# Chunks 2 and 3 of a gated recurrence take the split form and leave through memory, and three chunks' loads get an earliest time

## The chip, the cores and the metric

The kernel runs on one core of one Trainium2 chip. The metric is device time in microseconds for one execution. The unchanged kernel takes 480.79 us (median of three runs, 479.53 to 482.15). A core has TensorE (PE; its weight loads are shown as PEld), VectorE (DVE), ScalarE (ACT), GpSimd (POOL) and SyncE (SP), whose queue issues every DMA of this kernel. Each engine runs its own instructions in the order in which the program emits them.

## The reference

Two blocks follow each other. The first is a recurrence over 768 tokens for 4 batches x 8 heads, with a 48 x 48 state for each head:

```python
f = 1.0 / (1.0 + np.exp(-f_logit))
for t in range(S):
    state = f[:, :, t, :, None] * state + np.einsum('bhd,bhe->bhde', k[:, :, t], v[:, :, t])
    y[:, :, t] = np.einsum('bhd,bhde->bhe', q[:, :, t], state)
```

Its output, 3072 tokens x 384, is the input x of the second:

```python
a = x @ w1          # 384 x 1024
b = x @ w2
h = a * b @ w3      # 1024 x 1024
return (h @ w_out)  # 1024 x 384
```

q, k, v and f_logit arrive as 32-bit floats; the weights as 64-bit words.

## The kernel before

**Chunks.** The tokens are cut into 24 chunks of 128 (`NU`), six to a batch; four chunks make a block of 512 tokens, the unit of the FFN. For each chunk, `front` loads f, k and q (two DMAs of 96 KB each) and v (192 KB), takes the sigmoid on ScalarE, runs a forward and a backward product scan on VectorE, and scales q and k by them. TensorE then forms key-query products ("pairs"), ScalarE copies them to SBUF, GpSimd masks them (`affine_select`), TensorE multiplies by v and adds what the state gives, and the state is updated on VectorE.

**Two forms.** Below `NPE` (4) a chunk takes the whole form: 128 x 128 pairs, one select, values and state products over all 128 tokens (`first_values`, with the state copied by ScalarE into block-diagonal tiles `sb`), an update (`first_update`), and x^T made on TensorE with a permutation (`moved`, L737) and settled by ScalarE (L742). From `NPE` on a chunk takes the split form. It is cut at token 64: pairs are made within each half, so half as many products and two selects of 64 partitions each; the second half reads the state at token 64 (`mid`, L617 or L619), and the state at the chunk's end needs a second addition (L622) and the gain (L681). In this form the output leaves through memory: two DMAs write `ys` to a scratch tile in DRAM (`written`, L729) and a third gathers x^T from it (`gathered`, L732).

**Visits.** In the split form TensorE does a chunk in one visit, which also holds the pairs and the update of the next chunk. `begin` does those two for the first split chunk.

**Weights.** The 64-bit words of w1 and w2 (12 pieces of 512 KB), w_out (4 of 768 KB) and w3 (8 of 1 MB) are loaded by SP and turned into 32-bit floats: two operations on ScalarE (L1157, L1160), four on VectorE (L1163, L1164, L1168, L1174, the last of which is called the join). w3 and w_out are then folded into one 1024 x 384 matrix on TensorE (L1221), and after differences of these (L1253, L1267) later blocks use a seven-product scheme for halves. `fetch` describes a piece, `weights` all of them.

**The FFN.** Block 0 comes in parts: tokens of chunks 0 and 1 with the first half of w1 and w2, chunks 2 and 3 with the same, all four with the second half. A product takes one of four PSUM banks (pool "f"); ScalarE copies a's (L796) and VectorE multiplies b's by it (L801), which frees the bank.

**The order of the work.** Nothing is emitted directly. Every step is a task of a planner (`Plan`): an engine, an assumed cost, what it depends on, a priority (lower first), slots that it takes and frees. `order` repeatedly picks the task that can start earliest by the planner's own clock, then by priority, and the tasks are emitted in order of those starts. So each engine's order is the planner's; the chip's own times only decide how long it waits at each step. Loads take one of eight "lanes". SP is a queue in that order too: an issue that waits for data, as a gather does for its write, holds all later ones. Before the planner's time 35 (`FULL`), idle stretches of TensorE are filled with dummy products (`idle`, L268). A chunk's due time (`need`) is 0, 1, 2, 3 for the first four, then 60 and 14.5 more for each further one; f, k and q have priorities of due time minus 30, 29.5 and 29.

**The tail.** The last visit has no next chunk and makes one dummy transpose instead (L654).

Of the kernel before, what the change touches and what calls it, by code (L numbers as in the profile page):

```python
# [45 lines left out]
P = 128  # L46
C = 128
# [10 lines left out]
NB = B * S // TB  # L58
NLEAF = 6
NQ = HP * C  # L60
NPE = 4
NRAW = 3
NF = 4
DH = DM // 2
# [3 lines left out]
HIGH = float.fromhex("0x1.dffffep+16")  # L68
W = C // 2
FULL = 35.0  # L70
FLOOR = 2.0**-60
RANGE = 2.0**-40


class Plan:
# [13 lines left out]

        self.pools[name] = [None] * n  # L90

    def add(self, eng, cost, emit, deps=(), prio=0.0, takes=(), frees=(), lag=0.2, slack=0.0):


        t = {
            "eng": eng, "cost": cost, "emit": emit, "deps": [d for d in deps if d is not None], "prio": prio,
            "takes": list(takes), "frees": list(frees), "lag": lag, "slack": slack, "at": None, "end": None, "no": len(self.tasks),
        }
        self.tasks.append(t)
        return t  # L100

    def order(self):
        free, done, left = {}, [], list(self.tasks)
        enders = {}
        for t in self.tasks:
            for f in t["frees"]:
                enders.setdefault(id(f), []).append(t)

        def after(t, ds):

            if any(d["end"] is None for d in ds):
                return None
            return max([0.0] + [d["end"] + (d["lag"] + t["slack"] if d["eng"] != t["eng"] else 0.0) for d in ds])

        def places(t, name):

            ends = [(after(t, enders[id(h)]) if h else 0.0, i) for i, h in enumerate(self.pools[name])]
            return [e for e in ends if e[0] is not None]

        def start(t):  # L120

            waits, at = list(t["deps"]), free.get(t["eng"], 0.0)
            for name in t["takes"]:
                if name in self.pools:
                    ends = places(t, name)
                    if not ends:
                        return None
                    at = max(at, min(ends)[0])
                    continue
                n, taken = self.slots[name]  # L130
                if len(taken) >= n:
                    waits += enders[id(taken[-n])]
            ready = after(t, waits)
            return None if ready is None else max(at, ready)

        while left:
            at, _, _, t = min(
                ((at, t["prio"], t["no"], t) for t in left if (at := start(t)) is not None), key=lambda x: x[:3]
            )
            t["at"], t["end"] = at, at + t["cost"]  # L140
            free[t["eng"]] = t["end"]
            for name in t["takes"]:
                if name in self.pools:
                    t["got"] = min(places(t, name))[1]
                    self.pools[name][t["got"]] = t
                else:
                    self.slots[name][1].append(t)
            left.remove(t)
            done.append(t)
        return sorted(done, key=lambda t: (t["at"], t["no"]))  # L150
# [44 lines left out]
def ranged(ctx, tc, q, k, f_logit, v, w1, w2, w3, w_out, out, ident, w12, wc, left):  # L195
# [128 lines left out]
    def past(u, n, *names):  # L324
        return [tk[u - n][nm] for nm in names if u >= n and nm in tk[u - n]]

    def moves(n, size, rate, emit, deps, prio, late=0.0):


        for j in range(n):  # L330
            i = plan.add("SP", 0.45, (lambda: None) if j else emit, [d] if j else deps, prio - j * 1e-3, takes=["lane"], lag=0.6)
            d = i
            t = plan.add("DMA", size / n / rate, lambda: None, [i], prio - j * 1e-3, lag=1.3 + late, frees=[i])
        return t
# [5 lines left out]
    def front(u):  # L340

        s, t = st[u], tk[u]
        n0 = need(u)

        def load(dst, src):
            def emit():
                if dst is fs[0] and u == 0:

                    nc.sync.dma_start(dst[0:64], src[u].rearrange("two d n -> (two d) n")[0:64])
                    nc.sync.dma_start(dst[rows(1)], src[u, 1])  # L350
                    return
                for par in range(2):
                    nc.sync.dma_start(dst[rows(par)], src[u, par])
            return emit

        fu, qu, ku = (x[u if u < 4 else u % n] for x, n in ((fs, 2), (qs, 3), (ks, 2)))

        def free(n, *names):

            if u < 4:  # L360
                return []
            return asked[8:9] + [tk[u - n if u - n >= 4 else u % n][nm] for nm in names]

        t["lf"] = moves(2, 197, 250, load(fu, f_logit), free(2, "g"), n0 - 30)
        t["lk"] = moves(2, 197, 250, load(ku, k), free(2, "k"), n0 - 29.5)
        t["lq"] = moves(2, 197, 250, load(qu, q), free(3, "q"), n0 - 29)

        def load_v():
            s["v"] = at(12288 + NQ, DM) if u == 3 else loads.tile([P, DM], F32, name="vt")
            loaded(s["v"], u)  # L370

        t["lv"] = moves(
            1, 197, 320, load_v, [] if u == 3 else past(u, 4 if u in (4, 5, 6) else 3, "v", "s"),
            n0 - (28.2, 28.2, 28.2, 29.6, 12)[min(u, NPE)],
        )

        def gates():
            nc.scalar.activation(gate[u % 2][:, 0:NQ], fu, AF.Sigmoid)  # L378

        t["g"] = plan.add("ACT", 0.65, gates, [t["lf"]] + past(u, 2, "r") + past(u, 3, "G"), n0)  # L380
        if u % NCH and "G" in tk[u - 1]:
            tk[u - 1]["G"]["deps"].append(t["g"])

        def forward():
            s["P"] = one.tile([R, NQ], F32, name="fwd")
            nc.vector.tensor_tensor_scan(s["P"], gate[u % 2][:, 0:NQ], floor, 0.0, ALU.mult, ALU.max)  # L386

        t["p"] = plan.add("DVE", 1.25, forward, [t["g"]] + past(u, 1, "q", "i", "l"), n0)

        def last():  # L390
            nc.scalar.copy(lasts[:, u], heads(s["P"])[:, :, C - 1])  # L391

        t["l"] = plan.add("ACT", 0.2, last, [t["p"]], n0)

        def ends():
            nc.vector.reciprocal(heads(back)[:, :, C - 1], heads(s["P"])[:, :, C - 1])

        t["i"] = plan.add("DVE", 0.18, ends, [t["p"]] + past(u, 1, "r"), n0)

        def scale_q():  # L400
            s["Q"] = work3.tile([R, NQ], F32, name="Q")
            nc.vector.tensor_tensor(s["Q"], qu, s["P"], ALU.mult)

        t["q"] = plan.add("DVE", 0.7, scale_q, [t["p"], t["lq"]] + past(u, 3, "v", "a"), n0 + 0.1)

        def backward():
            s["R"] = one.tile([R, NQ], F32, name="bwd")
            nc.vector.tensor_tensor_scan(  # L408
                s["R"][:, ::-1], gate[u % 2][:, NQ:0:-1], back[:, ::-1], 0.0, ALU.mult, ALU.max
            )  # L410

        t["r"] = plan.add("DVE", 1.25, backward, [t["i"]] + past(u, 1, "k"), n0)

        def scale_k():
            s["K"] = work.tile([R, NQ], F32, name="K")
            nc.vector.tensor_tensor(s["K"], ku, s["R"], ALU.mult)

        t["k"] = plan.add("DVE", 0.7, scale_k, [t["r"], t["lk"]] + past(u, 2, "a", "t"), n0)
        if u in (2, 3):
            t["k"]["frees"].append(coming)  # L420
# [207 lines left out]
    def rest(u):  # L628
# [12 lines left out]
            t["s"] = plan.add("PE", 0.6, lambda: first_update(u), [t["e"], t["lv"]] + past(u, 1, "d"), n0 - 997)  # L641
        else:
            middle(u)
            more = u + 1 < NU
            after = tk[u + 1] if more else {}

            def visit():
                s["py"] = ps.tile([P, 2, NQ], F32, name="py")
                values(u, 1)
                if more:  # L650
                    pairs(u + 1)
                else:
                    s["pa"] = ps.tile([P, 2, NQ], F32, name="pa")
                    nc.tensor.transpose(out=s["pa"][:, 0, 0:R], in_=s["K"][:, 0:C], identity=ident[0:R, 0:R])  # L654
                values(u, 0)
                from_state(u)
                if more:
                    update(u + 1)
# [535 lines left out]
    def weights():  # L1194
        due = {(0, 0): 5.0, (1, 0): 8.0, (0, 1): 24.0, (1, 1): 26.0}
        pieces.update({key: [] for key in due})
        for half in range(2):
            for which, w in enumerate((w1, w2)):
                for kc in range(KM):
# [4 lines left out]
                        [(0, KH * P, w12_part(which, kc, c0), due[which, half] + 0.1 * kc, [])],  # L1204
                    )

        done = []
        for i in range(0, KF, 2):
            src = w_out[i * P : (i + 2) * P].rearrange("(kc p) c -> p kc c", p=P)
# [92 lines left out]

    setup()
    for u in range(NU):
        if u <= NPE:
            front(u)
        if u == NPE:
            turning(u)
            begin(u)
        if u >= NPE and u + 1 < NU:  # L1310
            front(u + 1)
            turning(u + 1)
        rest(u)
        if u == NPE - 1:
            weights()
        if u == NU - 1:
            looked = plan.add("DVE", 1.0, judge, [tk[i]["y"] for i in range(NU)], -20)
            sent = moves(1, 0.4, 250, told, [looked], 0, 20.0)
            judged = plan.add("DVE", 0.2, decided, [moves(1, 0.4, 250, heard, [sent], 0, 20.0)], -20)
# [349 lines left out]
```

## Time and profile before

| | |
|---|---|
| time, median of three runs | 480.79 us (479.53 to 482.15) |
| time of the profiled execution | 481.99 us |
| its span, first to last instruction | 480.3 us |
| mean granted TensorE clock | 0.997 |
| busy: PE, PEld | 466.2, 398.5 us |
| busy: DVE, ACT, POOL | 362.7, 141.2, 63.2 us |
| read from and written to HBM | 40.67 and 8.65 MB |
| chain that ended last, by engine | PE 78%, DMA 8%, DVE 7%, POOL 3% |

The profile is one execution. A line of a timeline gives the start and length of a group of like instructions, its engine, the line of the kernel, the tiles written and read, shapes, how often, and in brackets how long the engine had been idle before it and whom it waited for. A product of 32-bit floats appears as two passes on TensorE, so 72 passes are 36 products. TensorE counts as busy while a product is in flight, so a full row is not a TensorE at its peak. For loads, the queue rows give the issue; the landing is told apart from it.

### The profile page before, as it was taken

Reading aid. Unit: us, or ns where it says so; the run is one execution under the profiler, and the core shown is the slowest. Engines: PE = TensorE matmul, PEld = TensorE weight load, DVE = VectorE, ACT = ScalarE, POOL = GpSimd, SP = SyncE. Lnnn points to the kernel's source line nnn. Section 1 sums busy time; section 2 is a strip of 40 time slices with the busy share of each in tenths; the row PEclk is TensorE's granted clock in tenths of the full one; section 3 lists DMA queues with packets and bytes.
Section 4 is the critical chain, followed back from the end, with each engine's and each line's share of the span. In section 5 each row is a group of like instructions: output and inputs, shape, how many; then the busy total and the mean of one; then the engine's idle time right before and its main releaser. Section 6 shows DMA issues by size and latency. Waiting matters only on the chain.

```text
span 480.3 us, 11336 instructions
## 1 busy us (share of the span) xinstructions
PE 466.2 (97%) x4667; PEld 398.5 (83%) x4667; DVE 362.7 (76%) x706; ACT 141.2 (29%) x310; POOL 63.2 (13%) x88
## 2 busy tenths in 40 slices
PE   8799899999999899999999999999999999999995
PEld 6688644656799788899988889988899888889995
DVE  8999699999999889899899467367653667655541
ACT  4787356472313334333432210010100110110000
POOL 9300000013303224212431100000000000000000
PEclk9999999999999999999999999999999999999998
DMA  6899277843516664455631002100101000000011
GB/s 183 261 386 235 61 256 248 286 139 92 138 38 171 190 185 138 125 150 142 168 111 26 18 18 66 50 17 2 57 27 49 1 0 1 0 2 0 34 66 40
DMA packets 36622, 50.14 MB, mean 104 GB/s; under 512 B 4546, under 2 KB 26050, under 8 KB 35538
## 3 DMA queue, kind: packets, MB, share of 16 engines
q1 hardware_dynamic: 36562, 49.33, 34.1%
q8 instruction: 38, 0.62, 0.6%
q14 instruction: 22, 0.18, 0.1%
HBM read 40.67 MB, written 8.65 MB: 103 GB/s over the span
## 4 chain that ended last, share of the span: by engine, by line
PE 78%; DMA 8%; DVE 7%; POOL 3%; issue 2%; ACT 1%; SPq 0%; ACTq 0%; DVEq 0%; POOLq 0%
PE f L759 62%; PE f L1221 7%; PE py L513 2%; DMA vt<-in_v_dram 2%; DMA place<-in_w_dram 2%; PE pa L439 2%; DMA place<-in_w_out_dram 2%; PE f L453 2%; PE py L532 2%; PE pa L546 2%; DMA k<-in_k_dram 2%; DVE place L1168 1%; DVE place L1174 1%; POOL ab L304 1%; DVE ab L801 1%
## 5 line engine op out<-in xcount | busy, mean ns | idle before, releaser
L759 PE MATMUL f<-xt,w 128*128 128x256 f32 (+1 forms) x600 | 161.1, 397 | 3.4 <-ACT ab L796 1.9
L759 PEld LDWEIGHTS f<-xt,w 128*128 128x128 f32 x600 | 112.9, 190 | 29.1 <-issue 10.0
L759 PE MATMUL f<-place 128*128 128x192 f32 (+1 forms) x504 | 112.1, 349 | 0.1
L759 PEld LDWEIGHTS f<-place 128*128 128x128 f32 x504 | 87.7, 190 | 6.2 <-DVE place L1010 0.4
L569 POOL TENSOR_SCALAR_AFFINE_SELECT A<-A 64x512 f32<-64x512 f32 (+1 forms) x44 | 40.9, 929 | 117.3 <-ACT A L563 107.5
L1221 PE MATMUL f<-place 128*128 128x384 f32 x128 | 42.8, 489 | 0.2 <-DVE place L1174 0.2
L862 ACT COPY a<-f 128x256 f32<-128x256 f32 x36 | 13.4, 373 | 93.2 <-PE f L759 78.0
L1221 PEld LDWEIGHTS f<-place 128*128 128x128 f32 x128 | 23.8, 190 | 16.5 <-DVE place L1174 0.8
L759 PE MATMUL f<-xt,place 128*128 128x256 f32 x144 | 37.3, 382 | 0.0
L759 PE MATMUL f<-wc,ab 128*128 128x192 f32 x192 | 35.2, 327 | 0.0
L759 PEld LDWEIGHTS f<-wc,ab 128*128 128x128 f32 x192 | 32.0, 190 | 0.5
L408 DVE TENSOR_TENSOR_SCAN bwd<-gate,back 112x512 f32<-112x512 f32 x24 | 30.0, 1248 | 0.8
L386 DVE TENSOR_TENSOR_SCAN fwd<-gate,floor 112x512 f32<-112x512 f32 x24 | 29.6, 1232 | 1.2 <-ACT gate L378 0.3
L759 PEld LDWEIGHTS f<-xt,place 128*128 128x128 f32 x144 | 26.6, 189 | 3.3
L886 DVE TENSOR_TENSOR place<-f,a 128x256 f32<-128x256 f32 x36 | 15.2, 423 | 18.3 <-PE f L759 18.0
L1157 ACT ACTIVATE place<-place 128x512 f32<-128x512 f32 (+2 forms) x24 | 21.3, 887 | 7.8 <-DVE w L1174 3.8
L672 POOL TENSOR_TENSOR G<-lasts,gate 112x4 f32<-112x4 f32 x20 | 11.6, 580 | 88.1 <-ACT lasts L391 55.2
L1160 ACT ACTIVATE place<-place 128x512 f32<-128x512 uint32 (+2 forms) x24 | 21.1, 886 | 5.7 <-DMA place<-in_w_out_dram 5.7
L708 ACT ACTIVATE ys<-py 112x512 f32<-112x512 f32 x20 | 11.9, 596 | 34.4 <-PE py L532 34.4
L759 PE MATMUL f<-place,w 128*128 128x256 f32 x72 | 21.4, 379 | 0.0
L897 DVE TENSOR_TENSOR ab<-f,place 128x256 f32<-128x256 f32 x36 | 15.2, 423 | 6.2 <-PE f L759 5.3
L995 DVE TENSOR_TENSOR place<-ab 128x512 f32<-128x512 f32 x24 | 16.9, 703 | 3.5 <-PE f L759 3.5
(126 smaller groups left out, 641.1 us busy)
## 6 DMA issues: line engine op xcount, KB each, us to landing
place<-in_w_dram SPq DMA_DIRECT2D x8, 1024.0 KB, 4.9
place<-in_w_dram SPq DMA_DIRECT2D x12, 512.0 KB, 10.4
out_dram<-o SPq DMA_DIRECT2D x24, 192.0 KB, 1.9
q<-in_q_dram SPq DMA_DIRECT2D x46, 96.0 KB, 2.9
vt<-in_v_dram SPq DMA_DIRECT2D x23, 192.0 KB, 3.8
k<-in_k_dram SPq DMA_DIRECT2D x44, 96.0 KB, 2.3
f<-in_f_logit_dram SPq DMA_DIRECT2D x43, 96.0 KB, 2.5
yt<-ys SPq DMA_DIRECT2D x40, 96.0 KB, 2.6
```

The source lines that it names most:

```text
L386: nc.vector.tensor_tensor_scan(s["P"], gate[u % 2][:, 0:NQ], floor, 0.0, ALU.mult, ALU.max)
L408: nc.vector.tensor_tensor_scan(s["R"][:, ::-1], gate[u % 2][:, NQ:0:-1], back[:, ::-1], 0.0, ALU.mult, ALU.max)
L569: nc.gpsimd.affine_select(out=a, in_=a, pattern=pattern, compare_op=ALU.is_ge, fill=0.0, base=0, channel_multiplier=-1,)
L708: nc.scalar.activation(ys, py, AF.Copy, accum_out=ysum[:, u : u + 1])
L759: nc.tensor.matmul(out_, lhsT=lhs[i], rhs=rhs[i], start=start and i == 0, stop=i == len(lhs) - 1, skip_group_check=True,)
L862: nc.scalar.copy(q["a"], q["X"])
L886: nc.vector.tensor_tensor(ups["u3", k], q["Y"], q["a"], ALU.add)
L897: nc.vector.tensor_tensor(m if which else to(tok, half), q[bank_], m, ALU.add)
L995: nc.vector.tensor_tensor(abs_[j], x, y, op)
L1157: nc.scalar.activation(m, hi.bitcast(F32), AF.Abs)
L1160: nc.scalar.activation(lo.bitcast(F32), lo, AF.Copy, bias=2.0, scale=2.0**-51)
L1221: nc.tensor.matmul(w3s["p", jc], lhsT=w3s[jc][:, kc * P : kc * P + P], rhs=wos[:, kc], start=(kc == 0), stop=(kc == KF - 1),)
```

## The change

Chunks 2 and 3 take the split form: `NPE` becomes 2. They don't share visits: a new constant `SOLO` = 4 takes over what used to hang on the first split chunk. From chunk 4 on a visit includes the next chunk's pairs and update, as before; chunks 2, 3 and 4 each have a `begin` of their own, and the visits of 2 and 3 hold only their own values and state products. By the form's definition, x^T of these two goes through memory, and chunks 1 and 2 no longer copy their state into `sb`. The dummy transpose of the last visit goes.

Tasks get an earliest start, `since`. f, k and q of chunks 5, 6 and 7 get their due time minus 22 (`AHEAD`): 52.5, 67 and 81.5 by the planner's clock.

`weights` is cut in two: the part for w1 and w2 is described after chunk 0, the rest (`folding`) after chunk 3. The loads, their priorities and conditions stay.

```diff
-NPE = 4
+NPE = 2
+SOLO = 4
...
+AHEAD = 22.0
...
-            waits, at = list(t["deps"]), free.get(t["eng"], 0.0)
+            waits, at = list(t["deps"]), max(free.get(t["eng"], 0.0), t["since"])
...
-            i = plan.add("SP", 0.45, (lambda: None) if j else emit, [d] if j else deps, prio - j * 1e-3, takes=["lane"], lag=0.6)
+            i = plan.add("SP", 0.45, (lambda: None) if j else emit, [d] if j else deps, prio - j * 1e-3, takes=["lane"], lag=0.6, since=since)
...
-        t["lf"] = moves(2, 197, 250, load(fu, f_logit), free(2, "g"), n0 - 30)
-        t["lk"] = moves(2, 197, 250, load(ku, k), free(2, "k"), n0 - 29.5)
-        t["lq"] = moves(2, 197, 250, load(qu, q), free(3, "q"), n0 - 29)
+        since = n0 - AHEAD if 4 < u < 8 else 0.0
+        t["lf"] = moves(2, 197, 250, load(fu, f_logit), free(2, "g"), n0 - 30, since=since)
+        t["lk"] = moves(2, 197, 250, load(ku, k), free(2, "k"), n0 - 29.5, since=since)
+        t["lq"] = moves(2, 197, 250, load(qu, q), free(3, "q"), n0 - 29, since=since)
...
-            n0 - (28.2, 28.2, 28.2, 29.6, 12)[min(u, NPE)],
+            n0 - (28.2, 28.2, 28.2, 29.6, 12)[min(u, 4)],
...
-            more = u + 1 < NU
+            more = u + 1 < NU and u >= SOLO
...
                 if more:
                     pairs(u + 1)
-                else:
-                    s["pa"] = ps.tile([P, 2, NQ], F32, name="pa")
-                    nc.tensor.transpose(out=s["pa"][:, 0, 0:R], in_=s["K"][:, 0:C], identity=ident[0:R, 0:R])
                 values(u, 0)
...
+    def folding():
         done = []
...
-        if u <= NPE:
+        if u <= SOLO:
             front(u)
-        if u == NPE:
+        if NPE <= u <= SOLO:
             turning(u)
             begin(u)
-        if u >= NPE and u + 1 < NU:
+        if u >= SOLO and u + 1 < NU:
             front(u + 1)
             turning(u + 1)
         rest(u)
-        if u == NPE - 1:
+        if u == 0:
             weights()
+        if u == 3:
+            folding()
```

## The prediction

> **What bounds the kernel now.** I read the page first (shares and slices), then busy time by stretches of ten microseconds, then the timelines of TensorE, ScalarE and VectorE around the stage that the change touches, then the queue of the loads. From the page, busy time, and VectorE's row of the 40 slices (12 us each, in tenths):
>
> ```profile
> PE 466.2 (97%) x4667; PEld 398.5 (83%) x4667; DVE 362.7 (76%) x706; ACT 141.2 (29%) x310; POOL 63.2 (13%) x88
> DVE  8999699999999889899899467367653667655541
> ```
>
> TensorE is never idle for long, and VectorE is full until about 240 us but for one slice (48 to 60 us). The stretches (busy us of 10 on PE, PEld, DVE, ACT, POOL; clock; DMA share; GB/s):
>
> ```profile
> 30.00:40.00 10.00, 10.00 (x81) 9.03 (x76) 9.67 (x20) 9.26 (x19) 0.00 (x0) 1.00 1.01 318
> 40.00:50.00 10.00, 10.00 (x48) 8.81 (x47) 7.08 (x15) 5.31 (x9) 0.00 (x0) 1.00 0.87 206
> 50.00:60.00 10.00, 8.10 (x32) 5.81 (x32) 7.47 (x17) 4.42 (x9) 0.51 (x1) 1.00 0.19 50
> ```
>
> DMA is saturated to 40 us and nearly so to 48. TensorE's timeline: start, length, line, form, and in brackets the idle time before it.
>
> ```profile
> 33.26 1.60 PE L737 MATMUL f<-ys,ab 112*128 112x128 f32 x12
> 34.70 15.71 PE L759 MATMUL f<-xt,w 128*128 128x256 f32 x72
> 52.30 8.02 PE L759 MATMUL f<-xt,w 128*128 128x256 f32 x30 [1.90 <-ACT ab L796]
> ```
>
> From 34.70 the FFN runs without a break but for 1.90 us before 52.30. Two things set this stage, and neither is TensorE's attention work. VectorE joins the words of w1 and w2, and ScalarE, in order, stands behind a late load. From VectorE's timeline and then ScalarE's:
>
> ```profile
> 37.89 0.69 DVE L1174 CUSTOM_DVE_ANT_0 w<-place,w 128x1024 uint16<-128x1024 uint16 x1
> ...
> 52.28 0.42 DVE L801 TENSOR_TENSOR ab<-f,ab 128x256 f32<-128x256 f32 x1 [4.41 <-ACT ab L796]
> ```
>
> ```profile
> 51.12 0.88 ACT L1160 ACTIVATE place<-place 128x768 f32<-128x768 uint32 x1 [4.89 <-DMA place<-in_w_out_dram]
> 51.90 0.35 ACT L796 COPY ab<-f 128x256 f32<-128x256 f32 x1
> ```
>
> The sixth join (w2's last of the first half) ends at 38.58. The 72 passes take 15.71 us, 0.218 each; four w1 products are 24 passes, 5.24 us, so TensorE first needs w2 at 39.94. Part(0,2), 48 passes, ends at 45.17; 24 more fill the four banks by 50.4. Then it stands until ScalarE, held at L1160 for w_out's second piece, frees one. That piece was issued on SP's queue at
>
> ```profile
> 42.03 0.39 SPq L1138 DMA_DIRECT2D place<-in_w_out_dram  x1
> ```
>
> and landed at about 51.1, behind f and k of chunk 5 (issued at 40.11 and 41.02), with q of 5 and 6 (45.21) among its packets.
>
> **What the Trainium skill says.** "TensorE: Matmul & The Clock Gate", The mechanism: products that use different row groups run side by side. The trace agrees: 32 passes of L439 with 48 rows and 64 columns take 0.47 us, 15 ns each, where a pass of L429 (48 rows, 128 columns) takes about 69. "SBUF — State Buffer", Who interferes with whom: a VectorE instruction with two SBUF inputs contends with a GpSimd one that reads SBUF. It agrees: K at 22.20 (L416) took 1.40 us under the select of 21.90 to 23.05, 0.69 elsewhere. "DMA: Bandwidth & Descriptors", Two DMAs through the same engine are not ordered: a DMA that reads what another wrote must wait on the issuing engine for its completion. The waits agree (SP's queue; total, times, longest), and below it are the page's landings of both moves and the landing of the v loads issued between 12.8 and 28.6 us:
>
> ```profile
> SPq L732 <- DMA yt<-ys: 3.7, 4, 1.7
> ```
>
> ```profile
> yt<-ys SPq DMA_DIRECT2D x40, 96.0 KB, 2.6
> xt<-yt SPq DMA_DIRECT2D x20, 192.0 KB, 3.2
> ```
>
> ```profile
> DMA to landing us min/median/max: 9.3/9.6/10.0
> ```
>
> A move through memory costs 2.6 and 3.2 us on a free queue, but in the weight stage each landing takes nearly 10.
>
> **TensorE's work.** Removed for chunk 3, by starts: pairs 24.34 to 25.44 (1.10), values 29.25 to 30.27 (1.02), state 30.27 to 31.23 (0.96), update 32.66 to 33.26 (0.60), x^T 33.26 to 34.70 (1.44): 5.12 us. In its place stand the products of a later visit, whose ends are
>
> ```profile
> 119.43 0.45 PE L513 MATMUL py<-A,vt 64*64 64x64 f32 x16
> ...
> 121.41 0.91 PE L1221 MATMUL f<-place 128*128 128x384 f32 x2
> ```
>
> that is 1.98 us with the pairs and update of the next chunk, the same content as one chunk's own. The transposes stay. Gain 3.14 per chunk, 6.3 us for two, all before 34.70, where TensorE waits for joins anyway. Priced at nothing beyond an earlier start: w1's third join ends at 32.20, so without chunk 3's x^T in front TensorE could begin up to 2.5 us earlier, but then needs w2 at 37.4, before 38.58. At most 1.36 us (39.94 to 38.58) is to be had, if joins don't move.
>
> **VectorE.** They do move. The state of chunk 2 was 0.35 + 0.36 (L687, L688); it becomes 0.35 + 0.36 + 0.35 (L619, L622, L681): +0.35. Of chunk 3, the first two, 0.71, now come before the joins (its old pair ran at 53.22, after the gate of chunk 4). GpSimd's select was one of 1.1 us, and becomes two of 0.66 to 1.4, each a chance to block a two-input operation: 0 to 0.7 more per chunk. The sixth join moves to 39.64 at least and 41.0 at most, against a need of 39.94: -0.3 to +1.1. I take **+0.4**.
>
> **ScalarE** loses 3.2 us before 35: two pairs of L697 (2 x 0.71), two settles (2 x 0.48), two mask copies at 0.58 for 1.01. It runs ahead of VectorE here: nothing. The end-of-kernel transpose of L654 (0.3) goes: within the tail, nothing.
>
> **x^T through memory.** Chunk 3's Q would end near 24.9 (24.2 + 0.7 for chunk 2's state). Then pairs and update 1.1, ScalarE 0.6, selects 1.3 to 2.8, visit 1.1, ys 0.8: 29.8 to 31.3. The write lands 2.6 to 10 us later, the gather 3.2 to 5 after that: x(3) at 35.6 to 46.3. Part(2,4) needs it at 45.17 + 0.4 = 45.6. Cost 0 to 0.7; I take **+0.2**. The cover is part(0,2), 10.4 us of TensorE; without it every microsecond counts whole. Behind the waiting gather on SP stand w1/w2's last pieces, f and k of chunk 4, and w_out: these are late next.
>
> **The loads.** f and k of chunk 5 before w_out's second piece, q of 5 and 6 among it: 8 x 96 KB = 768 KB go out of this stage (f of 6 and 7, at 52.81, go later too). Into it come 4 x 96 + 2 x 192 = 768 KB of yt and xt. At 206 to 318 GB/s either is 2.5 to 3.8 us: a wash in bytes. What is left is when SP issues: a hold at the gathers costs, a lighter queue afterwards gives. I put the landing between 47 and 55, against 51.1. The stall then changes by -1.9 (TensorE is never held) to +4 (each microsecond of lateness is one of TensorE's). I take **-0.9**, since the transfer is issued with nothing of chunk 5 in front. Chunk 5's gate feeds a scan at 93.53 and its f would be on chip before 60: the later loads are priced at nothing, covered by some 30 us; past that cover lateness would stop VectorE.
>
> **After 55.** The products and folds are the same, at TensorE's pace; VectorE, which arrives together with it at fold two (83.69, 0.17 idle), has up to 4.4 us of freed idle time and 1.1 of added work: nothing. The order is planned anew from end to end, so stalls such as 1.37 us at 161.25 may go or new ones come: -1.5 to +1.5, taken at **-0.2**.
>
> Sum: 0.4 + 0.2 - 0.9 - 0.2 = -0.5 us on the profiled execution of 481.99 (span 480.3 and 1.7 around it), which is 1.2 above the median of 480.79. From the median: **480.3 us**.
>
> **Rivals.** A, the forecast: the saved TensorE time lies in front of VectorE's joins and buys nothing, the bytes cancel; 478.4 to 483.2. B, the late piece is the bound and the lighter queue frees it: landing by 49 takes all 1.9, the start up to 1.3 more, and 161.25's stall up to 1.4: 476.2 to 478.4, centre 477.5. For it: 4.41 us of idle VectorE time in the same place; against it: the same bytes come back. C, slower: SP stands at the gathers. With the write issued near 26 and landing near 36, SP holds from about 29; the last w2 piece slips from 29.88 to 36 or 37, w_out's second from 42.03 to about 46, its landing to 55: the stall is 1.9 + 4, time 484.8. It decides from a landing after 53.5 (2.4 us late). For it: the ten-microsecond landings; against it: the held queue drains, so what follows lands faster. D, the later loads are already late in the order and nothing moves there: then B fails, A or C stands; inside their chances.
>
> **Chances.** A 0.40, B 0.26, C 0.34; half a per cent, 2.4 us, is about what this kernel's measurement tells from no change. So faster 0.26, same 0.40, slower 0.34. The range takes in most of B and C and leaves about one in ten out at each end: 476.5 to 486; A alone, 478.4 to 483.2.
>
> **What would show it.** Right: L737 x24 for x48 with four more gathers and eight writes; first FFN product within a microsecond or two of 34.7; VectorE still over 9.5 of 10 to 48 us; ScalarE's wait on w_out between 3 and 7 us. Wrong: an FFN start below 32 (the joins were not the gate), that wait gone (B), or longer, with SP's waits for yt at 10 us in total (C); or a new stall of over 2 us past 55, which I price at nothing.

## The result and the profile after

The changed kernel takes **483.33 us** (median of 11 runs, 481.11 to 485.32), the kernel before 479.59 (11 runs, 478.15 to 482.15). The ratio is 1.0084 with a 95% interval of 1.0067 to 1.0102. Two later measurements of the same kernel gave 1.0099 (1.0080 to 1.0117) and 1.0110 (1.0091 to 1.0128). By the medians it is slower by 3.7, 4.6 and 5.6 us; the forecast was half a microsecond faster, 480.3 in a range of 476.5 to 486.

The profiled execution of the changed kernel took 481.11 us, the shortest of its eleven, with a span of 479.3, so it understates the loss; the first experiment below has a profile of a more usual one. Its mean granted clock, 0.999, is also the highest; the other ten have 0.990 to 0.996, where the kernel before has 0.997 or more in 49 of the 57 executions measured beside the experiments. So in most executions TensorE's clock probably fell, as in that next profile. Busy time and VectorE's slices of the profiled execution:

```profile
PE 465.2 (97%) x4804; PEld 396.8 (83%) x4804; DVE 363.2 (76%) x708; ACT 138.1 (29%) x304; POOL 64.0 (13%) x90
DVE  8998799999999889899899467367754667655441
```

Nothing here tells the two kernels apart. The stretches of ten microseconds do (length; busy us on PE, PEld, DVE, ACT, POOL; clock; DMA share; GB/s):

```profile
30.00:40.00 10.00, 9.90 (x104) 8.17 (x103) 9.65 (x20) 8.13 (x17) 0.19 (x1) 1.00 0.90 298
40.00:50.00 10.00, 6.91 (x33) 5.79 (x32) 7.05 (x17) 5.23 (x9) 0.47 (x1) 1.00 0.67 200
50.00:60.00 10.00, 10.00 (x41) 7.55 (x40) 8.76 (x18) 3.05 (x6) 0.00 (x0) 1.00 0.16 41
```

TensorE lost 3.1 us between 40 and 50, where it had been full; the hole at 50 to 60 is closed. TensorE's timeline:

```profile
32.75 10.80 PE L759 MATMUL f<-xt,w 128*128 128x256 f32 x48
46.63 13.60 PE L759 MATMUL f<-xt,w 128*128 128x256 f32 x55 [3.09 <-DVE w L1168]
```

The 48 passes of part(0,2) start at 32.75, 1.95 us earlier than before, and end at 43.55. Part(2,4) starts at 46.63. The view puts that wait down to VectorE's work on the words of the second half (L1168), but the join that part(2,4) needs, the sixth, was done at 38.91. What landed just before was chunk 3's gather. The view of tile xt from 30 to 50 us has the times from issue to landing of its two gathers (the smaller and the larger are chunk 2's and chunk 3's):

```profile
DMA to landing us min/median/max: 3.9/4.8/5.7
```

Chunk 3's was issued at 40.83 and landed at 46.54, 0.09 us before TensorE went on. SP's queue shows why it is so late (start, length, line, tiles, count):

```profile
32.67 2.69 SPq L729 DMA_DIRECT2D yt<-ys  x4
36.97 0.40 SPq L1138 DMA_DIRECT2D place<-in_w_out_dram  x1
37.41 1.37 SPq L355 DMA_DIRECT2D k<-in_k_dram  x2
38.89 0.39 SPq L732 DMA_DIRECT2D xt<-yt  x1
39.33 0.49 SPq L1138 DMA_DIRECT2D place<-in_w_out_dram  x1
39.86 0.93 SPq L355 DMA_DIRECT2D q<-in_q_dram  x2
40.83 0.47 SPq L732 DMA_DIRECT2D xt<-yt  x1
```

The last write landed at 38.84. The gather of chunk 3 was issued two microseconds later, behind chunk 2's gather, w_out's second piece (768 KB) and chunk 4's q, and took 5.7 us to land. That w_out piece landed at 44.98 in place of 51.04, and the old stall is gone:

```profile
48.47 0.90 ACT L1160 ACTIVATE place<-place 128x768 f32<-128x768 uint32 x1
```

stands without a wait. So this one execution lost the wait for the gather and won the earlier start and w_out's stall. At the second fold on TensorE it stands where the kernel before stood (the view of the chain, then the timeline of before):

```profile
83.74 5.43 PE f L1222 x16
```

```profile
83.69 5.43 PE L1221 MATMUL f<-place 128*128 128x384 f32 x16 [0.17 <-DVE place L1174]
```

The loss of the usual execution is what comes on top: a later landing, and a clock that falls.

### The profile page after: what moved, and what is told of

It reads as the page before. It is cut to its first block, busy times and chain, and to the rows that moved or that the text cites. A ratio compares the mean times of both kernels' runs of the same rounds, so it can differ in the third digit from the quotient of the medians.

```text
span 479.3 us, 11618 instructions
## 1 busy us (share of the span) xinstructions
PE 465.2 (97%) x4804; PEld 396.8 (83%) x4804; DVE 363.2 (76%) x708; ACT 138.1 (29%) x304; POOL 64.0 (13%) x90
## 4 chain that ended last, share of the span: by engine, by line
PE 86%; DVE 6%; DMA 4%; issue 1%; SPq 1%; POOL 1%; ACT 0%; DVEq 0%; POOLq 0%; ACTq 0%
PE f L759 68%; PE f L1222 7%; PE py L516 2%; DMA vt<-in_v_dram 2%; PE pa L442 2%; PE f L456 2%; PE py L535 2%; PE pa L549 2%; SPq L355 1%; DMA k<-in_k_dram 1%; DVE place L1268 1%; DVE w L1168 1%; DVE bwd L411 1%; DVE place L995 1%; DVE K L419 0%
## 5 line engine op out<-in xcount | busy, mean ns | idle before, releaser
L572 POOL TENSOR_SCALAR_AFFINE_SELECT A<-A 64x512 f32<-64x512 f32 (+1 forms) x46 | 42.3, 919 | 117.1 <-ACT A L566 114.9
L1222 PE MATMUL f<-place 128*128 128x384 f32 x128 | 42.8, 489 | 0.7 <-DVE place L1174 0.7
L1222 PEld LDWEIGHTS f<-place 128*128 128x128 f32 x128 | 23.8, 190 | 17.1 <-DVE place L1174 1.4
L708 ACT ACTIVATE ys<-py 112x512 f32<-112x512 f32 x22 | 13.1, 596 | 35.7 <-PE py L535 35.7
```

Source lines behind the costliest of these rows:

```text
L572: nc.gpsimd.affine_select(out=a, in_=a, pattern=pattern, compare_op=ALU.is_ge, fill=0.0, base=0, channel_multiplier=-1,)
L708: nc.scalar.activation(ys, py, AF.Copy, accum_out=ysum[:, u : u + 1])
L1222: nc.tensor.matmul(w3s["p", jc], lhsT=w3s[jc][:, kc * P : kc * P + P], rhs=wos[:, kc], start=(kc == 0), stop=(kc == KF - 1),)
```

## The experiments

Throughout, "fold two" is the start of the second group of sixteen passes of L1221 (L1222 after the change). From fold two to the end of the span every unfilled kernel here takes 395.1 to 396.6 us, but for one named below, so what happens before it decides. Ratios are to the kernel before on the same chip.

**The changed kernel again** (no edit).

> The changed kernel once more, for a second profile and a second ratio. The profiled execution of the first was its fastest (span 479.3 us; the other executions had 480.6 to 483.5), with TensorE standing 3.25 us at 43.2 for chunk 3's x^T, which landed at 46.54. Theory G (the gather of chunk 3 sets the restart, and its landing varies with the load of the queue): ratio 1.006 to 1.010, and a profile with a longer span shows this landing later than 46.5 and the stall longer by the same amount. Rival W (the weights' DMA and VectorE set the pace, the gather doesn't): the stall stays near 3.2 us whatever the span, and the difference lies elsewhere.

Measured: 484.37 us, ratio 1.0099. Its profile, an execution of 485.67 us:

```profile
48.25 8.08 PE L759 MATMUL f<-xt,w 128*128 128x256 f32 x23 [4.17 <-DVE w L1174]
```

The gather landed at 48.16, the stall grew by 1.1 us, and 23 passes now take 8.08 us where 55 took 13.60. The stretches of two microseconds show the granted clock (the last but two columns):

```profile
46.00:48.00 2.00, 0.00 (x0) 0.00 (x0) 1.25 (x2) 0.00 (x0) 0.00 (x0) 0.81 0.37 92
48.00:50.00 2.00, 1.75 (x4) 1.50 (x5) 0.00 (x0) 0.00 (x0) 0.00 (x0) 0.50 0.01 3
50.00:52.00 2.00, 2.00 (x6) 1.53 (x5) 0.00 (x0) 0.82 (x2) 0.00 (x0) 0.50 0.00 0
52.00:54.00 2.00, 2.00 (x6) 1.53 (x6) 0.19 (x1) 0.35 (x1) 0.00 (x0) 0.50 0.00 0
54.00:56.00 2.00, 2.00 (x11) 1.77 (x10) 1.60 (x4) 0.37 (x1) 0.00 (x0) 0.98 0.00 0
```

TensorE had stood 4.17 us; its clock was halved from 47.26 to 54.09. It worked 5.84 us of that, which is 2.9 us lost; from restart to fold two it took 39.98 us against 37.11 in the first profile, 2.87 more. Fold two is at 88.23, 4.5 us later than there: 1.6 of it the later landing, 2.9 the clock.

**The later loads alone**, on the kernel before.

```diff
+        since = n0 - AHEAD if 4 < u < 8 else 0.0
+        t["lf"] = moves(2, 197, 250, load(fu, f_logit), free(2, "g"), n0 - 30, since=since)
...
```

> The kernel before with the earliest times for f, k and q of chunks 5 to 7 alone; chunks 2 and 3 keep the whole form and x^T on TensorE. My forecast's part: w_out's second piece lands near 46 to 48 in place of 51.04, the 1.9 us stall at 50.4 goes, ratio 0.995 to 0.998. Rival (the loads are hidden anyway, the stall is re-made elsewhere): ratio 0.999 to 1.001.

Measured: 479.29 us, ratio 1.0000 (0.9987 to 1.0014), the rival's number. Yet the stall is gone, as forecast:

```profile
34.79 41.48 PE L761 MATMUL f<-xt,w 128*128 128x256 f32 x144
```

That is one row without a break to the first fold. Fold two comes at 82.14, 0.9 us before the second profile of the kernel before (83.07, last but one below): TensorE is 1.5 us ahead at the first fold, and in front of the second stand a transpose and the wait for a join that ends at 82.05. About a microsecond is left at fold two, and the medians show less.

**The change without the later loads.**

```diff
-        since = n0 - AHEAD if 4 < u < 8 else 0.0
+        since = 0.0
```

> The changed kernel without the earliest times: chunks 2 and 3 in split form with x^T through memory, loads of chunks 5 to 7 as early as before. Theory G: the gathers wait behind still more bytes (768 KB more in the queue before 48 us), x(3) lands 1 to 4 us later than in the changed kernel, ratio 1.010 to 1.018. Rival W: ratio as the changed kernel's, 1.006 to 1.010.

Measured: 486.05 us, ratio 1.0141 (1.0119 to 1.0162), within what the gather's theory expected. In the profile, its shortest execution, the gather was issued at 41.47 and landed at 48.22, which is 0 to 1.7 us later than in the three profiles of the changed kernel, where 1 to 4 were expected. The view itself names the gather here:

```profile
48.31 11.96 PE L759 MATMUL f<-xt,w 128*128 128x256 f32 x47 [4.85 <-DMA xt<-yt]
```

The clock was halved for 3.4 us, fold two came at 86.99. The later loads are not what costs: without them the change is worse (1.0099 with them on the same chip).

**The memory path alone**: whole form, later loads, x^T of chunks 2 and 3 through memory.

```diff
+                if u < NPE:
+                    to = s["yt"].rearrange("(b two d) c -> two d b c", two=2, d=D)[half]
...
-        if u < NPE:
+        if u < 2:
             t["z"] = plan.add("PE", 1.6, moved, [t["y"]], n0 - 996, takes=["f"], frees=[moving])
```

> The kernel before with the earliest times and with x^T of chunks 2 and 3 through memory, but these chunks in the whole form (no split, no state at token 64). Theory G: the same late gather as in the changed kernel, ratio 1.005 to 1.012. Rival S (the split form costs: VectorE's extra state operations and the two selects in front of the joins): ratio 0.995 to 1.002, the loss is the form's.

Measured: 487.88 us, ratio 1.0169 (1.0144 to 1.0193), more than the theory expected. Here SP stood from the loads of f to chunk 2's gather, whose write landed at 38.29, chunk 3's writes were issued behind that, and the last gather was issued at 42.82 (SP's queue, then TensorE):

```profile
33.46 0.83 SPq L354 DMA_DIRECT2D f<-in_f_logit_dram  x2
38.34 0.39 SPq L736 DMA_DIRECT2D xt<-yt  x1
...
42.82 0.43 SPq L736 DMA_DIRECT2D xt<-yt  x1
```

```profile
51.04 9.29 PE L763 MATMUL f<-xt,w 128*128 128x256 f32 x29 [7.01 <-issue]
```

It landed at 50.95, and the clock was halved for 10.2 us. So the path through memory is enough for the loss, without the split form; by another order in SP's queue, it makes more of it.

**The gathers first.** In the changed kernel, k and q of chunk 4 and w_out's pieces are held until after both gathers. TensorE's, VectorE's and GpSimd's orders are untouched; ScalarE takes up w_out's pieces later.

```diff
-        since = n0 - AHEAD if 4 < u < 8 else 0.0
-        t["lf"] = moves(2, 197, 250, load(fu, f_logit), free(2, "g"), n0 - 30, since=since)
+        since = n0 - AHEAD if 4 < u < 8 else 37.7 if u == 4 else 0.0
+        t["lf"] = moves(2, 197, 250, load(fu, f_logit), free(2, "g"), n0 - 30, since=since if u > 4 else 0.0)
...
-        ld = moves(1, total, 380, load, held, prio, max(0.0, 3.5 - 1.2 * load_no) if load_no < 4 * KM else 3.0)
+        ld = moves(1, total, 380, load, held, prio, max(0.0, 3.5 - 1.2 * load_no) if load_no < 4 * KM else 3.0, 37.7 if a == 2 else 0.0)
```

> The changed kernel with one change in SP's order: k and q of chunk 4 and the pieces of w_out not before 37.7 by the planner's clock, which puts both gathers in front of them; TensorE's order is the same. In the changed kernel's two profiles chunk 3's gather was issued at 40.8 and 41.2, behind w_out's second piece, and landed at 46.5 and 48.2. Theory G: it is issued near 39.3 with only chunk 2's gather in front, lands at 41.5 to 43, TensorE stands under 0.5 us at 43 and its clock never falls; ratio to before 0.990 to 0.998. Rival W: the stall is re-made by w_out's later landing or by VectorE's joins, ratio 1.003 to 1.010.

Measured: 477.84 us against 478.96, ratio **0.9974** (0.9958 to 0.9990): faster than both kernels. SP's queue and TensorE:

```profile
38.23 0.92 SPq L732 DMA_DIRECT2D xt<-yt  x2
39.24 0.95 SPq L1138 DMA_DIRECT2D place<-in_w_out_dram  x2
```

```profile
32.88 29.57 PE L759 MATMUL f<-xt,w 128*128 128x256 f32 x116
```

The second gather, issued at 38.72 just after its data had landed (38.66), landed at 41.99, 3.27 us later. TensorE runs through, its clock stays whole, fold two is at 80.38. w_out's second piece lands at 48.59 here and nothing waits for it. Moving two gathers past four loads and two pieces of w_out is worth 1.1 to 1.4% of the kernel, the whole loss and a little more.

**The stall filled**: ten dummy products in front of the first product of part(2,4).

```diff
+                    if n == 0 and (c0, jc, which) == (2, 0, 0):
+                        idle(10)
```

> The changed kernel with ten dummy products (20 passes, 4.3 us of TensorE) in front of the first product of chunks 2 and 3; nothing else moves, the gather is as late as before. In the changed kernel's second profile the clock was at one half from 47.26 to 54.09 after TensorE had stood 4.34 us; in the first (3.25 us) it never fell. Theory C (a good part of the loss is the clock that falls when TensorE stands too long): the clock stays whole in the profile, TensorE restarts at 47 to 48.5, ratio 1.000 to 1.005. Rival (the stall alone): ratio as the changed kernel's, 1.007 to 1.011, or more by the filler's tail.

Measured: 483.17 us, ratio 1.0076 (1.0052 to 1.0100), the rival's number. The clock stayed whole in the profile, but the filler ended at 47.5 while the gather had landed at 46.33, and 2.35 us were lost later, at 163.10. That is another gather of x^T, which landed at 163.01 in this trace. So the number says little of the clock. (The expectation's 4.34 and 3.25 us are the waits of 4.17 and 3.09, counted from 0.17 us earlier.)

**The stall filled less** (`idle(7)`), **and the changed kernel a third time**, on one chip.

> The changed kernel with seven dummy products (3.0 us) in front of the first product of chunks 2 and 3 in place of ten, so that they end by 46.3, about when the gather lands, and TensorE stands under 2.5 us after them. Theory C: the granted clock stays as high as the kernel before's (0.997 to 0.999 in the mean of its executions), and the time is 0.5 to 2.5 us under the changed kernel's of the same chip, the rest of the loss staying. Rival: no difference to the changed kernel (under 0.4 us).

> The changed kernel on the same chip as the filled one, to compare the two: ratio 1.007 to 1.011; mean clock 0.990 to 0.996 in most executions; in the profile TensorE stands 3 to 5.5 us from 43.2, until chunk 3's x^T has landed.

Measured: 484.40 (ratio 1.0128, 1.0097 to 1.0159) and 484.13 (1.0110). The filler kept the mean clock at 0.997 to 0.999 in four of six executions, against 0.990 to 0.995 in all six without it, but the time didn't fall: the expected 0.5 to 2.5 us were missed. The two profiles show where the gain of the stage went (the filled one first):

```profile
47.12 15.35 PE L759 MATMUL f<-xt,w 128*128 128x256 f32 x59 [0.70 <-DMA xt<-yt]
```

```profile
48.29 13.95 PE L759 MATMUL f<-xt,w 128*128 128x256 f32 x52 [4.83 <-issue]
```

From restart to fold two they take 37.13 and 38.74 us: the halved clock, 3.4 us of it, costs 1.6 there, and a landing later by 1.1 the rest of 2.8 us at fold two. The filled kernel then loses about 2 us behind fold two (397.6 against 395.6), among it 1.35 at 161.80 (a gather that landed at 161.71) and 0.97 at 187.32. The clock's price is shown within the stage. That it is a part of the total time follows from the first two profiles of the changed kernel, which differ by 4.5 us at fold two and by 0.1 behind it; it was not shown by a faster kernel.

**Split form, x^T on TensorE**: a second permutation, ten products for each chunk.

```diff
...
-        if u < NPE:
-            t["z"] = plan.add("PE", 1.6, moved, [t["y"]], n0 - 996, takes=["f"], frees=[moving])
+        if u < SOLO:
+            t["z"] = plan.add("PE", 1.6 if u < NPE else 2.6, moved, [t["y"]] + split * (u >= NPE), n0 - 996, takes=["f"], frees=[moving])
```

> The changed kernel with x^T of chunks 2 and 3 on TensorE by a second permutation (10 products of 128 columns for each chunk in place of 6, ten small copies on ScalarE to build it); the split form and the later loads stay. Theory G: no stall near 43 and no fall of the clock; 2 x 2.4 us of TensorE come back in front of it; ratio 0.994 to 1.001. Rival S (the split form itself costs): ratio 1.004 or more.

> The split form with x^T on TensorE once more, for a profile: its first profiled execution was its fastest (481.37 us against a median of 483.15). If what the median has over that is a stall that TensorE meets in front of the folds (1.7 us at 82.3 in the first profile), this profile shows it at 2.5 to 4 us; otherwise the place of the rest is open.

Measured: 483.15 us, ratio 1.0081 (1.0057 to 1.0104); the second profile's execution took 483.48. There was no stall near 43, as expected, but the time was the rival's. In both profiles fold two waits 1.56 us, for VectorE and for a transpose planned in front of it, and stands at 84.08 and 84.28; and in both TensorE stops in the middle of a visit (the second profile):

```profile
249.74 0.33 PE L565 MATMUL pa<-vt,kt 64*48 64x48 f32 x10 [1.78 <-issue]
```

The second profile differs from the first here: after this stop the clock was halved from 250.59 to 254.01, and it took 397.5 us from fold two to the end (395.6 in the first). So what this execution has over the first lies there, and not in front of the folds. A mean clock of 0.994 in three of the five other executions of the first measurement makes the same likely for these, but they have no profile. What makes the stop is open: in both profiles it ends 0.02 us or less after a load of v has landed, and 1.4 to 1.5 us after the end of a packet of the queue that the profile calls "instruction". No run tells these apart or rules out a third cause. This kernel moves too much at once (the planner laid out everything behind it anew) to tell what the split form costs.

**Whole form, through memory, gathers first.** The edits of the last memory kernel and of the gathers together.

> The memory-only kernel (whole form, x^T of chunks 2 and 3 through memory, later loads) with the gathers in front of k and q of chunk 4 and of w_out, as in the run with the gathers first. Theory G: TensorE doesn't stand at 43, ratio 0.993 to 1.001, near the split form's 0.9974; what differs between the two is the form's own cost and gain. Rival S (the form matters by itself): over 0.4% away from 0.9974.

Measured: 478.76 us, ratio 1.0000 (0.9983 to 1.0018). TensorE stood 0.48 us at 43.63, fold two was at 80.78. Beside 0.9974 for the split form: 0.26%, with intervals that overlap, under the 0.4% that the rival named. The form itself is worth a microsecond or nothing; no cost of it shows.

**The kernel before again** (no edit).

> The kernel before once more, for a second profile. The first profiled execution took 481.99 us, the median over all rounds is 479.8. If the 1.9 us stall at 50.4 for w_out's second piece is in every execution, this profile shows it at 1.5 to 2.5 us; if it belongs to that execution alone, it is under 0.5 us and the span is 477 to 478.5.

Measured: 480.14 us, span 478.4, fold two at 83.07. The stall on w_out is there, a little under the expected size:

```profile
51.70 10.60 PE L759 MATMUL f<-xt,w 128*128 128x256 f32 x36 [1.29 <-ACT ab L796]
```

Before fold two, the third profile of the change adds up against this one: part(0,2) ends earlier (43.46 for 45.24, -1.8), the wait for the gather (43.46 to 48.29, +4.8), the clock (+1.6), the old stall gone (-1.3), the wait at fold two 0.74 in place of 0.16 (+0.6): +3.9, where fold two went from 83.07 to 87.03.

## Why the prediction failed

**TensorE's work** was placed rightly and priced nearly so: for chunk 3, 2.33 us of products stand where 5.12 stood, 2.8 us less (forecast 3.14), in front of the FFN, and it bought only an earlier start. The start moved by 1.95 us where I allowed 1.36 at most before the joins' delay, for two reasons. I read the need for the sixth join four passes too early: the trace has the 29th pass waiting for it, not the 25th (it starts at 38.96, the join ends at 38.91; the 29th started at 40.75 before). That is some 0.8 us more to be had. And **the joins** moved less than I took: the sixth ended 0.33 us later (forecast 1.1 to 2.4). Chunk 3's K, which had shared its time with a select (1.40 us at 22.20), now ran alone (0.69 at 22.34), and so did a step of the words (L1168, 1.58 us at 27.77, 0.68 at 27.93). So the term of +0.4 was about -1.7 by the end of part(0,2). My comparison of L439 with L429 does not show what row groups do: L429's passes use two row groups as well and start in pairs (two at 9.54); L439's start in fours (112.02 to 112.04), with half the columns, since the chunk's halves also go to different rows of the output.

**The step that failed is "x^T through memory", cost 0 to 0.7, taken at 0.2.** It measured 3.1, 4.2 and 4.8 us in the three profiles. My bound for the landing, 35.6 to 46.3, was passed only just in the best profile (46.54) and by 1.9 us in the others. The write was not the fault, by luck: the last one was issued at 35.06, later than the 31.3 at which I had it ready at the latest, and landed after 3.8 us where I had allowed 10. With my 3.2 to 5 us the gather would have landed at 42.0 to 43.8, about when part(0,2) ended. But I took those from the write's landing and left out that the gather has a place in SP's order: it was issued 2.0 to 2.3 us after its data were there, behind 768 KB of w_out and chunk 4's q, and landed 5.7 to 7.4 us later. Of a moved step I had counted what stands behind it on the queue, and not what stands in front of it. And the need had come forward to 43.5 from the 45.6 that I used: a gain that I rated as small turned the cover into a stall. That this step is the cause is shown by the gathers put first: TensorE's order is the same, the gather lands at 41.99, and the stall and the loss are gone.

**The clock was no term of the sum.** I priced a stall at its length. "TensorE: Matmul & The Clock Gate", What's actually happening, in the Trainium skill, says that after an idle window of about 3.4 us the array runs at half clock until it has been busy for such a window, and that the windows run freely. The lengths agree: the stretches at half clock, the lows, last 3.41, 6.83 and 10.24 us, one, two and three such windows, after 4.83, 4.17 and 7.01 us without work, and none came after 3.09. In these profiles a window that was only partly worked in did not end the low, as its edges show: after 4.83 us TensorE restarted 0.11 us into a window and the low ended with it; after 4.17 us it restarted 1.0 us into one (estimated by counting 3.41 us on from 47.26 and back from 54.09) and had to work through the next as well. The idle side agrees less: after 7.01 us without work the low began 2.42 us after the last product, less than a window. The price is half of the time worked in the low, 1.6 to 2.9 us on top of the wait.

**The loads and w_out's stall** (-0.9, range -1.9 to +4): the piece landed six microseconds earlier in the first profile and three to four in the others, and the stall of 1.3 to 1.9 went whole. "A wash in bytes" was the wrong measure, because the order in the queue decides: f and k of chunk 5 had stood in front of that piece, and now the gather of chunk 3 stood behind it. What w_out gained, the gather lost, and TensorE waited for the gather.

**"After 55, nothing"** held from fold two on (395.6 us, against 395.4 and 396.6 in the kernel before). In front of it, VectorE was held too: it stood 2.81 us before 49.57 for a product of TensorE, and fold two then waits 0.75 us for a join where it had waited 0.17. That is a term of +0.6 that I did not have.

**The sum.** For the two first profiles it is -1.7 (start), +3.1 (gather), -1.9 (w_out's stall), +0.6 (fold two) and -1.0 behind fold two, -0.9 in all; the forecast was -0.5. So the best execution met the size by luck: two terms were wrong by two to three microseconds in opposite directions. In the usual one the gather costs 4.2 to 4.8, the clock 1.6 to 2.9 more, and the gains, 3.1 to 3.6 us, cover only a part of that.

**The rivals.** C had the sign and nearly the size (484.8) but another mechanism: SP standing at the gathers and w_out landing at 55. SP's waits for the writes grew only from 3.7 to 4.9 us in all and w_out came early; what was late was x^T itself. Only the memory path in the whole form shows SP held for 4 us, as C had it. B's w_out gain was real at 50, and the kernel with the gathers first takes 477.84, near B's centre of 477.5, but that is a coincidence of levels: it is 1.1 us faster than the kernel before on its chip, where B had 3.3. D was wrong: with the later loads alone, w_out's second piece was issued at 39.74 in place of 42.03 and 43.51.

## What to carry to other kernels

When a value leaves TensorE for a path through memory, follow both of its transfers in the issuing queue: count what is issued in front of each at the time when its data are ready, and compare the landing with a need that the same change may have moved forward. In a stage where the DMA queue is full, put such small transfers ahead of bulk loads that are needed later: here that order alone was worth over 1%. And ask of a stall of TensorE whether the clock can fall in it: here it fell after 4.17 us and more and not after 3.09 (and once after 1.78, so this is no threshold). Where it falls, the stall costs its length plus half of the time that TensorE then works at half clock.

## What the runs showed that was not expected

The clock fell just after a stop of 1.78 us in the middle of a visit in one execution (250.59 to 254.01), and not in another of the same kernel with the same stop; what else it takes is open.

A gather of x^T also stops TensorE later, for 0.3 to 2.4 us between 157 and 168 us in ten of the fourteen profiles, the kernel before among them. The wait of 1.37 us that the forecast named at 161.25 is put down to ScalarE by the view, but the trace has a gather landing at 161.16. With the gathers first it is 1.32 us at 157.88, landing 157.79. In all ten TensorE goes on 0.09 us after the landing.

And taking away the stall before 52 (1.3 to 1.9 us in the kernel before) did not show in the median of the kernel with the later loads alone: 479.29 against 479.76, ratio 1.0000.
